# Attention blocks of two to five key tiles, sized freely within each unit, eleven tiles of probabilities, and two steps moved up

## The chip, the cores and the metric

The kernel runs on one core of a Trainium2 chip. The metric is the time of one execution on the device in microseconds (us), the median of several runs. Engine names are those of the profile: PE is TensorE's matmuls and PEld its weight loads, DVE is VectorE, ACT is ScalarE, POOL is GpSimd, SP is SyncE, which here only issues DMAs.

## What is computed

The reference takes 2048 tokens of width 512, normalises each (xn), and computes two branches from xn: attention with 32 heads of 16 columns, and a gated feed-forward network of hidden width 1792. The second branch gates the first.

```python
x = A_x
xn = _layernorm(x, axis=-1)
s = _A_ref(xn, A_wqkv, A_wo)          # softmax(q k^T / 4) v, 32 heads, then @ wo
g = _silu(_B_ref(xn, B_w_gate, B_w_up, B_w_down))   # (silu(xn wg) * (xn wu)) @ wd
return x + s * g
```

## The kernel before

**Prologue.** For each of four blocks of 512 tokens the kernel normalises, transposes and projects to queries, keys and values, and stores the results to DRAM (q_d, k_d, v_d; the normalised, transposed tokens to xt_d). Each float32 operand that needs accuracy is split into a high and a low part, so a product costs three matmuls (high by high, high by low, low by high).

**Attention.** A unit is one group of four heads with one block of 512 queries; there are 32 units, each over 16 key tiles of 128 keys. For one key tile and one j of two (j picks two of the four heads), two score matmuls run side by side on the two 64-row halves of the array and fill score[j], 128 keys x 2 heads x 512 queries in PSUM; ScalarE takes the exponential of it into a tile pr of probabilities (pool ppool, 8 buffers, 4 KB a partition each). So a key tile has two score pairs and two exponentials. The value products (function values) multiply the probabilities by v into the one PSUM tile acc, four heads in four column groups of 32; acc is summed over the 16 key tiles of a unit. Then finish transposes acc on VectorE (L423, in normalise), divides by the sum of probabilities, and for every second group transposes again (L437) and stores to o_d.

**Blocks.** Key tiles are worked in blocks. In a block of k tiles there are 2k score pairs. Between the second and the third score pair the value products of the block before are issued (values(prev)); after the last key tile of a unit, finish follows them. The last score tile of each block writes its second half to the PSUM tile spare, and its exponential is done in two halves (L876, L877), so that the next block's score can start earlier; all others are one instruction (L874). Before, every unit has six blocks, four of three key tiles and two of two (SIZES = {2: 2, 3: 4}), in an order that plan chooses for most of the units.

**Fills.** Into the blocks the kernel weaves the matmuls of the feed-forward network and of the output projection as fills: one call of both is a pair of matmuls on the two 64-row halves, into bankx and banky. The fills come from a queue of generators: ffn for four token blocks (per block 14 tiles of 24 fills for the gate and up weights, then 4 tiles of 24 and 4 of 18 for the down weights), the projection of the last token block's first three parts for two row tiles (EARLY, nine fills each), then project_out for the other three token blocks (twelve fills a tile). plan returns, for each block, its number of key tiles and how many fills follow each score pair from the third on; a tile's end is always a block's end. A tile's results go through ACT and DVE (L264 to L266, split_hidden) or DVE alone (L283, L287).

**Around them.** catch_up carries out work put off in the list after: store_gate (tanh on ACT, a multiplication on DVE, a store by POOL), next_out and load_gates. out_steps loads and splits the operands of the output projection in the last units; its loads of a unit's last part depend on the block's number, now, being past a unit's start. load_gate loads the gate and x rows of the last four row tiles, gate_rest multiplies and adds them for two of these tiles ahead of the end (L407, L408). Key and value chunks of the next head group (load_k, load_v, four key tiles a chunk) are loaded at the end of a block in the last unit of a group, as the chunks come free; queries are loaded a unit ahead. After the last unit the code from L900 normalises it in two halves and finishes the projection of the last token block (L917).

The order on each engine is written out by hand; each engine works its queue in order and waits on semaphores.

Of the kernel before, what the change touches and what calls it, by code (L numbers as in the profile page):

```python
# [38 lines left out]
RING = NB  # L39
DC = D // HALF  # L40
LIMIT = 160.0
SIZES = {2: 2, 3: 4}
FIRST = (4, 0, 4, 3, 3, 2, 2)
EARLY = 2
EPS = 1e-5
# [4 lines left out]
def plan():  # L50

    sizes = sorted(SIZES)
    least, most = {2: 6, 3: 12}, {2: 12, 3: 16}
    left = []
    for i in range(2 * NB):
        nf = GROUPS[i % 2].stop - GROUPS[i % 2].start  # L60
        left += [3 * DC] * nf + [3 * nf] * NT
    left = left[2:]
    blocks = [(3, sum(FIRST)), (2, 3 * DC - sum(FIRST))]
    rest = [3 * (DT - 1)] * EARLY + [3 * DT] * (NT * (NB - 1))
    ends = H // 4 * NB * sum(SIZES.values()) - len(rest)
    whole = tuple(SIZES[k] for k in sizes)
    start = tuple(SIZES[k] - sum(b[0] == k for b in blocks) for k in sizes)
    layers = [{(0, left[0], start): (0, None)}]
    for _ in range(len(blocks), ends):
        new = {}  # L70
        for state, (cost, _) in layers[-1].items():
            tile_no, rem, kinds = state
            kinds = kinds if any(kinds) else whole
            for i, k in enumerate(sizes):
                if not kinds[i]:
                    continue
                for n in range(least[2] // 2, min(most[k], rem) + 1):
                    if n == rem:
                        after = tile_no + 1, left[tile_no + 1] if tile_no + 1 < len(left) else 0
                    elif rem - n >= least[2] // 2:  # L80
                        after = tile_no, rem - n
                    else:
                        continue
                    if after[0] < len(left) or len(layers) + len(blocks) == ends:
                        key = after + (kinds[:i] + (kinds[i] - 1,) + kinds[i + 1:],)
                        c = cost + 100 * max(0, least[k] - n) + abs(n - 4 * k)
                        if key not in new or c < new[key][0]:
                            new[key] = c, (state, k, n)
        layers.append(new)
    state = min((v[0], s) for s, v in layers[-1].items() if s[0] == len(left))[1]  # L90
    kinds = state[2]
    middle = []
    for layer in layers[:0:-1]:
        state, k, n = layer[state][1]
        middle.append((k, n))
    blocks += middle[::-1]
    order = []
    while len(order) < len(rest):
        order += [k for i, k in reversed(list(enumerate(sizes))) for _ in range(kinds[i])]
        kinds = whole  # L100
    blocks += zip(order, rest)
    parts = []
    for k, n in blocks:
        m = 2 * k - 2
        parts.append((k, [0, 0] + [n // m + (i < n % m) for i in range(m)]))
    parts[0] = 3, list(FIRST[1:])
    return parts
# [3 lines left out]
def tile_block(ctx: ExitStack, tc: tile.TileContext, x, wqkv, wo, w_gate, w_up, w_down, out):  # L111
# [239 lines left out]
    def out_steps():  # L351
        for b in range(NB - 1):
            if b not in stage and (len(queue) <= NB, 0 in stage and now > stage.get(0, now), ready[0] == DT)[b]:
                for c in range(DT - 1):
                    load_out(b, c)
                stage[b] = now
            if b in stage and b < 2 and (b, 1) not in stage and now > (u0 + b) * steps:
                load_out(b, DT - 1)
                stage[b, 1] = now
            if b in stage and (b, 2) not in stage and now > stage[b] and (b < 2 or len(queue) <= 2):  # L360
                splits.extend((b, c) for c in range(DT - 1))
                stage[b, 2] = now
                for t in range(0 if b else NT):
                    load_gates(t)
            if (b, 1) in stage and (b, 5) not in stage and now > stage[b, 1]:
                splits.insert(0 if not b else len(splits), (b, DT - 1))
                stage[b, 5] = now
        for _ in range(min(2, len(splits))):
            b, c = splits.pop(0)
            split_o(lhs[b, c], parts_o[b, c])  # L370
            ready[b] += 1
# [34 lines left out]
    def gate_rest(t):  # L406
        dve.scalar_tensor_tensor(facc[:, t], facc[:, t], 0.5, gate[t], op0=ALU.mult, op1=ALU.mult)  # L407
        dve.tensor_add(facc[:, t], facc[:, t], last[t])  # L408


    def values(item):
        u, tiles, probs = item
        for i, kt in enumerate(tiles):
            v = vst[(u // NB * NB + kt // CT) % RING]
            for h in range(4):
                mm(acc[h * 32:h * 32 + DH + 1], v[:, kt % CT, h * (DH + 1):(h + 1) * (DH + 1)],  # L416
                   probs[2 * i + h // 2][:, h % 2], start=kt == 0, stop=kt == KT - 1, skip_group_check=True)
# [14 lines left out]
    def finish(u):  # L432
        g, b = divmod(u, NB)
        normalise(u, 0, TB)
        if g % 2:
            o2 = late.tile([P, TB], F32, tag="o1", name="o2")
            dve.transpose(o2, on[b])  # L437
            if g < NG - 1 or b < 2:
                (pool if g < NG - 1 else sp).dma_start(o_d[g // 2, b], o2)
            else:  # L440
                whole = hh.rearrange("p f j t -> p (f j) t")
                lhs[b, DT - 1] = whole[:, 2 * (DT - 1)], whole[:, 2 * DT - 1]
                split_o(lhs[b, DT - 1], o2)
                ready[b] += 1

    settled = mybir.DependencyInfo(mybir.DependencyClass.Sync, mybir.DependencyReason.DATA)
    units = NG * NB
    steps = sum(SIZES.values())

    u0 = units - NB + 1  # L450

# [17 lines left out]
            given += 1  # L469

    blocks = plan()

    def blocked():
        return not queue or queue[0][0] is not None and ready[queue[0][0]] < DT
# [345 lines left out]
        made()  # L820


    ppool = ctx.enter_context(tc.tile_pool(name="ppool", bufs=8))
    att = ctx.enter_context(tc.tile_pool(name="att", bufs=1))
    late = ctx.enter_context(tc.tile_pool(name="late", bufs=1))
    spool = ctx.enter_context(tc.tile_pool(name="spool", bufs=1, space=PSUM))
# [19 lines left out]
    for u in range(units):  # L846
        g, b = divmod(u, NB)
        q = qst[u % 2]
        kt = 0
        for i in range(steps):  # L850
            now = u * steps + i
            size, parts = blocks[now]
            tiles = range(kt, kt + size)
            kt += size
            probs = []
            if not now:
                fill(FIRST[0])
            for n in range(2 * size):
                t, j = tiles[n // 2], n % 2
                if n == 2:  # L860
                    catch_up()
                    if prev:
                        values(prev)
                        if prev[1][-1] == KT - 1:
                            finish(prev[0])
                k, kc = kst[(g * NB + t // CT) % RING], t % CT

                room, whole = score[j], n < 2 * size - 1
                for h in range(2):
                    r = slice(h * HALF, h * HALF + NROW)  # L870
                    mm(room[:, h] if whole or not h else spare, k[r, j, kc * P:(kc + 1) * P], q[r, j], start=True, stop=True)  # L871
                pr = ppool.tile([P, 2, TB], F32, tag="pr", name="pr")
                if whole:
                    made = act(pr, room, AF.Exp, scale=0.25)  # L874
                else:
                    act(pr[:, 0], room[:, 0], AF.Exp, scale=0.25)  # L876
                    made = act(pr[:, 1], spare, AF.Exp, scale=0.25)  # L877
                exps.append(made)
                if n == 1 and now:
                    tc.add_manual_dep(exps[-1].ins, exps[-3].ins.name, settled, reason="order of the slots' writes")  # L880
                probs.append(pr)
                fill(parts[n])
            if prev and prev[0] // NB + 1 < NG and prev[0] % NB == NB - 1:
                done = prev[1][-1] + 1
                while len(coming) < done // CT:
                    load_k(prev[0] // NB + 1, len(coming))
                    load_v(prev[0] // NB + 1, len(coming))
                    coming.append(now)
                if done == KT:
                    coming.clear()  # L890
            prev = u, tiles, probs
            if i == 0 and u + 1 < units:
                load_q(u + 1)
                load_shift(u + 1)
            out_steps()
            if now == (units - 1) * steps + 1:
                load_gate()
            if 0 <= now - (units - 1) * steps - 4 < EARLY:
                gate_rest(now - (units - 1) * steps - 4)
    values(prev)  # L900
    fill(total)
    catch_up()
# [76 lines left out]
```

## Time and profile before

| what | value |
|---|---|
| median of 3 runs | 1419.76 us (1419.52 to 1419.98) |
| the profiled execution, whole | 1419.49 us |
| its span, first to last instruction | 1417.7 us |
| mean granted TensorE clock | 0.999 |
| attention and fills, 157 to 1403 us | PE busy 1245.45 of 1246.00 us, ACT 1031.38, DVE 452.80 |
| after 1403 us | PE busy 8.49 of 15.00 us, DVE 11.02 |

Busy time is the time in which an engine has an instruction running. Matmuls overlap: a record lasts about 0.39 us, while a pair starts every 0.23 us, so a busy PE may still lose time between starts. The chain of waits gives the distances. A row of the timeline gives the start, the length, the engine and the line of one or several like instructions, and in square brackets the idle time before it and what ended that.

### The profile page before, as it was taken

Reading aid. Unit: us, or ns where it says so; the run is one execution under the profiler, and the core shown is the slowest. Engines: PE = TensorE matmul, PEld = TensorE weight load, DVE = VectorE, ACT = ScalarE, POOL = GpSimd, SP = SyncE. Lnnn points to the kernel's source line nnn. Section 1 sums busy time; section 2 is a strip of 40 time slices with the busy share of each in tenths; the row PEclk is TensorE's granted clock in tenths of the full one; section 3 lists DMA queues with packets and bytes.
Section 4 is the critical chain, followed back from the end, with each engine's and each line's share of the span. In section 5 each row is a group of like instructions: output and inputs, shape, how many; then the busy total and the mean of one; then the engine's idle time right before and its main releaser. Section 6 shows DMA issues by size and latency. Waiting matters only on the chain.

```text
span 1417.7 us, 26890 instructions
## 1 busy us (share of the span) xinstructions
PE 1409.6 (99%) x11197; PEld 817.8 (58%) x11197; DVE 543.2 (38%) x900; ACT 1112.7 (78%) x1427; POOL 90.2 (6%) x102
## 2 busy tenths in 40 slices
PE   9999999999999999999999999999999999999998
PEld 7787655555555555555555555555555555555554
DVE  6643344213423343145224431433244412433645
ACT  6733588888888888878888887888888878888874
POOL 4200100000000000000000000000000000000243
PEclk9999999999999999999999999999999999999999
DMA  7878542042274320242724311256224202313542
GB/s 244 262 247 271 137 95 64 22 96 61 61 159 108 105 75 25 57 110 67 166 65 104 91 39 35 65 124 152 81 64 132 58 12 61 84 54 128 173 153 99
DMA packets 127645, 149.15 MB, mean 105 GB/s; under 512 B 12577, under 2 KB 79649, under 8 KB 126750
## 3 DMA queue, kind: packets, MB, share of 16 engines
q1 hardware_dynamic: 122206, 126.72, 34.7%
q0 software_dynamic: 4880, 20.12, 3.9%
q8 instruction: 90, 1.47, 0.5%
q10 hardware_dynamic: 432, 0.52, 0.1%
q14 instruction: 37, 0.30, 0.1%
HBM read 107.46 MB, written 40.11 MB: 104 GB/s over the span
## 4 chain that ended last, share of the span: by engine, by line
PE 88%; DVE 1%; ACT 0%; issue 0%; DVEq 0%
PE acc L416 32%; PE bankx L235 31%; PE score L871 19%; PE banky L235 5%; PE spare L871 0%; ACT pr L874 0%; PE banky L917 0%; PE score L917 0%; DVE facc L408 0%; DVE o L423 0%; PE spare L917 0%; DVE y L924 0%; DVE y L389 0%; DVE facc L407 0%; DVE y L240 0%
## 5 line engine op out<-in xcount | busy, mean ns | idle before, releaser
L874 ACT ACTIVATE pr<-score 128x1024 f32<-128x1024 f32 x832 | 816.7, 1033 | 201.8 <-PE score L871 190.0
L416 PE MATMUL acc<-pr,vst 128*17 128x512 f32 x4096 | 476.8, 594 | 0.6 <-DVE o L423 0.6
L871 PE MATMUL score<-qst,kst 50*128 50x512 f32 x1856 | 398.2, 418 | 0.0
L871 PEld LDWEIGHTS score<-qst,kst 50*128 50x128 f32 x1856 | 192.9, 184 | 216.4 <-ACT pr L874 153.5
L235 PE MATMUL bankx<-fx,guh 64*128 64x512 f32 x896 | 289.0, 392 | 0.1
L235 PE MATMUL banky<-fx,guh 64*128 64x512 f32 x896 | 289.1, 392 | 0.0
L416 PEld LDWEIGHTS acc<-pr,vst 128*17 128x17 f32 x4096 | 100.5, 97 | 256.4 <-issue 254.5
L235 PE MATMUL banky<-wd,hh 64*128 64x512 f32 x672 | 189.3, 392 | 0.0
L235 PE MATMUL bankx<-wd,hh 64*128 64x512 f32 x672 | 189.3, 392 | 0.0
L235 PEld LDWEIGHTS bankx<-fx,guh 64*128 64x128 f32 x896 | 166.8, 186 | 31.8 <-DVEq L788 0.5
L265 DVE SCALAR_TENSOR_TENSOR ga<-th,bankx 128x512 f32<-128x512 f32 x56 | 38.5, 688 | 371.8 <-ACT th L264 371.8
L235 PE MATMUL banky<-fx,gul 64*128 64x512 f32 x448 | 175.4, 391 | 0.0
L235 PE MATMUL bankx<-fx,gul 64*128 64x512 f32 x448 | 175.3, 391 | 0.0
L235 PEld LDWEIGHTS banky<-fx,guh 64*128 64x128 f32 x896 | 166.8, 186 | 3.4
L235 PEld LDWEIGHTS bankx<-wd,hh 64*128 64x128 f32 x672 | 125.0, 186 | 22.8
L235 PEld LDWEIGHTS banky<-wd,hh 64*128 64x128 f32 x672 | 125.0, 186 | 3.3
L876 ACT ACTIVATE pr<-score 128x512 f32<-128x512 f32 x192 | 114.8, 598 | 11.9 <-PE spare L871 1.8
L877 ACT ACTIVATE pr<-spare 128x512 f32<-128x512 f32 x192 | 114.1, 595 | 0.0
L235 PEld LDWEIGHTS bankx<-fx,gul 64*128 64x128 f32 x448 | 82.8, 185 | 16.0
L235 PEld LDWEIGHTS banky<-fx,gul 64*128 64x128 f32 x448 | 82.9, 185 | 1.9
L626 PE MATMUL ps<-xt,wh 128*128 128x512 f32 x256 | 81.0, 397 | 0.1
L871 PE MATMUL spare<-qst,kst 50*128 50x512 f32 x192 | 75.7, 394 | 0.0
(169 smaller groups left out, 1197.4 us busy)
## 6 DMA issues: line engine op xcount, KB each, us to landing
gur<-in_B_w_gate_dram SPq DMA_DIRECT2D x56, 256.0 KB
gur<-in_B_w_up_dram SPq DMA_DIRECT2D x56, 256.0 KB
wdr<-in_B_w_down_dram SPq DMA_DIRECT2D x56, 256.0 KB
kst<-k_d SPq DMA_DIRECT2D x192, 64.0 KB
qst<-q_d SPq DMA_DIRECT2D x192, 64.0 KB
fx<-xt_d SPq DMA_DIRECT2D x24, 512.0 KB
q_d<-parts SPq DMA_DIRECT2D x16, 512.0 KB
k_d<-parts SPq DMA_DIRECT2D x16, 512.0 KB
```

What stands on the lines that cost most here:

```text
L235: mm(bank, lhs[h], rhs[h], start=start, stop=stop)
L265: dve.scalar_tensor_tensor(ga, th, 1.0, bankx, op0=ALU.add, op1=ALU.mult)
L416: mm(acc[h * 32:h * 32 + DH + 1], v[:, kt % CT, h * (DH + 1):(h + 1) * (DH + 1)], probs[2 * i + h // 2][:, h % 2], start=kt == 0, stop=kt ...
L626: mm(ps, w, a[:, c], start=n == 0, stop=n == 3 * DT - 1)
L871: mm(room[:, h] if whole or not h else spare, k[r, j, kc * P:(kc + 1) * P], q[r, j], start=True, stop=True)
L874: made = act(pr, room, AF.Exp, scale=0.25)
L876: act(pr[:, 0], room[:, 0], AF.Exp, scale=0.25)
L877: made = act(pr[:, 1], spare, AF.Exp, scale=0.25)
```

## The change

Six things are changed.

1. plan is rewritten. Blocks may have 2, 3, 4 or 5 key tiles, any mix that adds up to 16 in a unit and leaves no single tile over. A dynamic programme over (key tiles done, fills done) minimises 1400 per block, 1000 for each fill that a block of k tiles has below 6(k-1), and a small term for uneven shares; a block takes at most 6k+6 fills, at most what is left in the fill tile, and the fills keep within 45 of an even pace. The first two blocks stay. The two nine-fill tiles get two blocks, (2,2), (3,2) or (3,3), whichever is cheapest, and the last two units keep 3, 3, 3, 3, 2, 2.
2. The loop over a unit's blocks and three conditions count from begin, a list of the first block of each unit, in place of multiples of steps.
3. ppool has 11 buffers in place of 8.
4. The size of the scratch memory that the build sets aside for dynamic DMAs is set to 4096 bytes, where no size was given.
5. Where the block before ended a unit, values and finish are issued ahead of catch_up; elsewhere catch_up stays first.
6. gate_rest for the two tiles runs after the fourth and fifth block of the last unit, in place of the fifth and sixth; load_gate stays after the second.

```diff
--- before.py
+++ after.py
@@ -39,7 +39,8 @@
 RING = NB
 DC = D // HALF
 LIMIT = 160.0
-SIZES = {2: 2, 3: 4}
+SIZES = (2, 3, 4, 5)
+LAST = (3, 3, 3, 3, 2, 2)
 FIRST = (4, 0, 4, 3, 3, 2, 2)
 EARLY = 2
 EPS = 1e-5
@@ -53,54 +54,46 @@
 
 
 
-    sizes = sorted(SIZES)
-    least, most = {2: 6, 3: 12}, {2: 12, 3: 16}
-    left = []
+    ends = [0]
     for i in range(2 * NB):
         nf = GROUPS[i % 2].stop - GROUPS[i % 2].start
-        left += [3 * DC] * nf + [3 * nf] * NT
-    left = left[2:]
-    blocks = [(3, sum(FIRST)), (2, 3 * DC - sum(FIRST))]
-    rest = [3 * (DT - 1)] * EARLY + [3 * DT] * (NT * (NB - 1))
-    ends = H // 4 * NB * sum(SIZES.values()) - len(rest)
-    whole = tuple(SIZES[k] for k in sizes)
-    start = tuple(SIZES[k] - sum(b[0] == k for b in blocks) for k in sizes)
...
+        for n in [3 * DC] * nf + [3 * nf] * NT:
+            ends.append(ends[-1] + n)
+
+    ends = [n - ends[1] for n in ends[2:]]
+    first = [(3, sum(FIRST)), (2, ends[0] - sum(FIRST))]
+    units = H // 4 * NB
+    start, stop = sum(k for k, _ in first), (units - 2) * KT
+    pace = (ends[-1] - ends[0]) / (stop - start)
+    short = lambda k, n: 1000 * max(0, 6 * (k - 1) - n)
+    ways = {at: {} for at in range(start, stop + 1)}
+    ways[start][ends[0]] = 0, None
+    for at in range(start, stop):
+        room = KT - at % KT
+        for done, (cost, _) in ways[at].items():
+            rem = next((n for n in ends if n > done), done) - done
+            for k in SIZES:
+                for n in [rem] + list(range(3, rem - 2)):
+                    to = at + k, done + n
+                    if not n or n > 6 * k + 6 or k > room or room - k == 1:
                         continue
-                    if after[0] < len(left) or len(layers) + len(blocks) == ends:
-                        key = after + (kinds[:i] + (kinds[i] - 1,) + kinds[i + 1:],)
-                        c = cost + 100 * max(0, least[k] - n) + abs(n - 4 * k)
-                        if key not in new or c < new[key][0]:
-                            new[key] = c, (state, k, n)
-        layers.append(new)
-    state = min((v[0], s) for s, v in layers[-1].items() if s[0] == len(left))[1]
-    kinds = state[2]
-    middle = []
-    for layer in layers[:0:-1]:
-        state, k, n = layer[state][1]
-        middle.append((k, n))
-    blocks += middle[::-1]
-    order = []
-    while len(order) < len(rest):
-        order += [k for i, k in reversed(list(enumerate(sizes))) for _ in range(kinds[i])]
-        kinds = whole
-    blocks += zip(order, rest)
+                    if abs(to[1] - ends[0] - (to[0] - start) * pace) > 45:
+                        continue
+                    c = cost + 1400 + short(k, n) + 4 * abs(n - 4.1 * k)
+                    if to[1] not in ways[to[0]] or ways[to[0]][to[1]][0] > c:
+                        ways[to[0]][to[1]] = c, (at, done, k, n)
+
+    rest = [3 * (DT - 1)] * EARLY
+    pairs = {4: (2, 2), 5: (3, 2), 6: (3, 3)}
+    cost = lambda r: ways[stop - r][ends[-1]][0] + sum(short(k, n) for k, n in zip(pairs[r], rest))
+    r = min((r for r in pairs if ends[-1] in ways[stop - r]), key=cost)
+    middle, step = [], ways[stop - r][ends[-1]][1]
+    while step:
+        middle.insert(0, step[2:])
+        step = ways[step[0]][step[1]][1]
+    rest += [3 * DT] * (NT * (NB - 1))
     parts = []
-    for k, n in blocks:
+    for k, n in first + middle + list(zip(pairs[r] + 2 * LAST, rest)):
         m = 2 * k - 2
         parts.append((k, [0, 0] + [n // m + (i < n % m) for i in range(m)]))
     parts[0] = 3, list(FIRST[1:])
@@ -354,7 +347,7 @@
                 for c in range(DT - 1):
                     load_out(b, c)
                 stage[b] = now
-            if b in stage and b < 2 and (b, 1) not in stage and now > (u0 + b) * steps:
+            if b in stage and b < 2 and (b, 1) not in stage and now > begin[u0 + b]:
                 load_out(b, DT - 1)
                 stage[b, 1] = now
             if b in stage and (b, 2) not in stage and now > stage[b] and (b < 2 or len(queue) <= 2):
@@ -445,7 +438,6 @@
 
     settled = mybir.DependencyInfo(mybir.DependencyClass.Sync, mybir.DependencyReason.DATA)
     units = NG * NB
-    steps = sum(SIZES.values())
 
     u0 = units - NB + 1
 
@@ -469,6 +461,13 @@
             given += 1
 
     blocks = plan()
+
+    begin, n = [], 0
+    for i, (k, _) in enumerate(blocks):
+        if n % KT == 0:
+            begin.append(i)
+        n += k
+    begin.append(len(blocks))
 
     def blocked():
         return not queue or queue[0][0] is not None and ready[queue[0][0]] < DT
@@ -820,7 +819,7 @@
         made()
 
 
-    ppool = ctx.enter_context(tc.tile_pool(name="ppool", bufs=8))
+    ppool = ctx.enter_context(tc.tile_pool(name="ppool", bufs=11))
     att = ctx.enter_context(tc.tile_pool(name="att", bufs=1))
     late = ctx.enter_context(tc.tile_pool(name="late", bufs=1))
     spool = ctx.enter_context(tc.tile_pool(name="spool", bufs=1, space=PSUM))
@@ -847,8 +846,7 @@
         g, b = divmod(u, NB)
         q = qst[u % 2]
         kt = 0
-        for i in range(steps):
-            now = u * steps + i
+        for now in range(begin[u], begin[u + 1]):
             size, parts = blocks[now]
             tiles = range(kt, kt + size)
             kt += size
@@ -857,12 +855,14 @@
                 fill(FIRST[0])
             for n in range(2 * size):
                 t, j = tiles[n // 2], n % 2
-                if n == 2:
+                if n == 2 and prev and prev[1][-1] == KT - 1:
+                    values(prev)
+                    finish(prev[0])
+                    catch_up()
+                elif n == 2:
                     catch_up()
                     if prev:
                         values(prev)
-                        if prev[1][-1] == KT - 1:
-                            finish(prev[0])
                 k, kc = kst[(g * NB + t // CT) % RING], t % CT
 
                 room, whole = score[j], n < 2 * size - 1
@@ -889,14 +889,14 @@
                 if done == KT:
                     coming.clear()
             prev = u, tiles, probs
-            if i == 0 and u + 1 < units:
+            if now == begin[u] and u + 1 < units:
                 load_q(u + 1)
                 load_shift(u + 1)
             out_steps()
-            if now == (units - 1) * steps + 1:
+            if now == begin[units - 1] + 1:
                 load_gate()
-            if 0 <= now - (units - 1) * steps - 4 < EARLY:
-                gate_rest(now - (units - 1) * steps - 4)
+            if 0 <= now - begin[units - 1] - 3 < EARLY:
+                gate_rest(now - begin[units - 1] - 3)
     values(prev)
     fill(total)
     catch_up()
@@ -962,7 +962,7 @@
     import concourse.bacc as bacc
     from concourse.bass_utils import run_bass_kernel_spmd
 
-    nc = bacc.Bacc("TRN2", target_bir_lowering=False, num_devices=1)
+    nc = bacc.Bacc("TRN2", target_bir_lowering=False, num_devices=1, dynamic_dma_scratch_size=4096)
     arrays, args = {}, []
     for name in _INS:
         a = np.asarray(inputs[name])
```

More of the change, by code (lines that the diff above doesn't have):

```diff
@@ L68, in plan @@
[L68 to L82, printed above, removed]
-                        continue
-                    if after[0] < len(left) or len(layers) + len(blocks) == ends:
-                        key = after + (kinds[:i] + (kinds[i] - 1,) + kinds[i + 1:],)
-                        c = cost + 100 * max(0, least[k] - n) + abs(n - 4 * k)
-                        if key not in new or c < new[key][0]:
-                            new[key] = c, (state, k, n)
-        layers.append(new)
```

## The prediction

> **What bounds the kernel now.** I read the page's first part, then the groups, then the chain of waits in order of time, then PE, ACT and DVE row by row.
>
> ```profile
> span 1417.7 us, 26890 instructions
> PE 1409.6 (99%) x11197; PEld 817.8 (58%) x11197; DVE 543.2 (38%) x900; ACT 1112.7 (78%) x1427; POOL 90.2 (6%) x102
> L874 ACT ACTIVATE pr<-score 128x1024 f32<-128x1024 f32 x832 | 816.7, 1033 | 201.8 <-PE score L871 190.0
> L876 ACT ACTIVATE pr<-score 128x512 f32<-128x512 f32 x192 | 114.8, 598 | 11.9 <-PE spare L871 1.8
> ```
>
> TensorE has work 99% of the span, ScalarE 78%, and ScalarE's idle time ends with a score matmul: TensorE's own order of work is the bound, so only fewer or quicker TensorE steps, or a shorter tail, can shorten the run. The 192 instructions of L876 are one per block (the last score tile of a block is split in two halves), so the kernel runs 192 blocks. How a block is spent, by the chain of waits (start us, length us, what):
>
> ```profile
> 614.50 0.47 PE score L871 x4
> 614.97 2.70 PE acc L416 x24
> 617.67 0.43 PE score L871 x2
> 618.10 0.23 PE bankx L235
> ...
> 620.20 0.47 PE score L871 x4
> 620.67 1.84 PE acc L416 x16
> 622.51 0.43 PE score L871 x2
> 622.94 0.23 PE bankx L235
> ```
>
> A pair of matmuls on the two row halves (one fill, or one score pair) takes 0.23 us. The value products take 2.70 us for three key tiles (x24) and 1.84 for two (x16): 0.86 a tile, and 2.70 − 3 × 0.86 = 0.12 that does not depend on the number of tiles. The first score pair after them takes 0.43 where a pair takes 0.23: 0.20 more. So one change-over from row halves to value products and back costs **0.32 us per block**, in short blocks and long ones alike. That is 192 × 0.32 = 61 us of TensorE's time which computes nothing.
>
> **The change, part by part.**
>
> *Number of blocks.* Every fill, score and value product stays; only the grouping changes. I count the new blocks by hand. The first two (3 and 2 tiles) stay, and so do the last twelve (LAST is the old 3,3,3,3,2,2 in units 30 and 31), with two more ahead of them for the nine-fill tiles. Between lie 512 − 5 − 32 − K' key tiles and 2016 − 24 − 24 = 1968 fills in 70 tiles of 24 and 16 of 18 (each ends with a block). The new planner charges 1400 per block, and 1000 for every fill below 6(k−1) in a block of k tiles. With no fill short, the k−1 of the blocks in a tile of 24 add up to 4 at most (one block of 5, or 4+2, or 3+3), and in a tile of 18 to 3. Over all of them that is 1968/6 = 328 = key tiles − blocks. With K' = 4 (the pair 2,2) there are 471 key tiles, so 471 − 328 = 143 blocks. Saving one more block needs six fills short, 6000 against 1400, and the pair (3,2) in place of (2,2) saves one block for three short fills, 3000: neither pays. That the units' ends at 16 tiles can be met without loss I take from the freedom of 3+3, 4+2 and 5; I did not enumerate it, and allow ±4 blocks. Together 2 + 143 + 2 + 12 = 159 blocks, **33 fewer: 33 × 0.32 = 10.6 us**. A page of the Trainium skill, TensorEngine Tiling (Array Packing), Key Properties, says that changing the tiling mode drains the engine. The trace agrees as far as it goes, with the 0.12 and 0.20 above; the page gives no price.
>
> *ScalarE under longer blocks.* Where the old plan mixed three and four fills between two score pairs, the new one has three almost everywhere, so a score pair comes each 4 × 0.233 = 0.933 us. Can ScalarE follow?
>
> ```profile
> 606.42 0.60 ACT L876 ACTIVATE pr<-score 128x512 f32<-128x512 f32 x1
> 606.91 0.59 ACT L877 ACTIVATE pr<-spare 128x512 f32<-128x512 f32 x1
> 607.60 1.94 ACT L874 ACTIVATE pr<-score 128x1024 f32<-128x1024 f32 x2
> ```
>
> Two exponentials end 1.94 us after the first starts, one lasts 1.03, so they start 0.91 apart; the two halves of the split tile start 0.49 apart, 0.98 together. A block of five therefore needs 7 × 0.91 + 0.98 = 7.35 us for the eight tiles that TensorE hands over in 8 × 0.933 = 7.46. It fits, by 0.1 us. The bounds from rows are 0.91 (no cost) and 1.03 (the whole length, no overlap); I take 0.91, which is the distance itself. ScalarE: Activation LUTs in the Trainium skill (What ACT_TABLE_LOAD costs) speaks against this: 186 ns + 0.833 ns an element less 93 ns of overlap makes an estimate of 0.946 us, over 0.933, some 7 us lost over the run. The 0.91 above disagrees, and the sum goes by it.
>
> *The nine-fill blocks.* What too few fills cost is seen where the old plan put nine fills into blocks of three:
>
> ```profile
> 1314.32 2.77 PE L416 MATMUL acc<-pr,vst 128*17 128x512 f32 x24
> ...
> 1318.76 0.39 PE L871 MATMUL score<-qst,kst 50*128 50x512 f32 x2
> ...
> 1319.57 0.49 PE L871 MATMUL score<-qst,kst 50*128 50x512 f32 x1
> ...
> 1320.49 0.99 PE L871 MATMUL score<-qst,kst 50*128 50x512 f32 x4
> 1321.40 2.77 PE L416 MATMUL acc<-pr,vst 128*17 128x512 f32 x24
> ```
>
> With two fills the pairs should stand 0.70 apart; they stand 0.81 and 0.92. The block lasts 7.08 us; 3 × 0.86 + 15 × 0.233 + 0.32 = 6.40 is its price without waits, so it lost 0.68. The other such block, of the same shape, is counted alike. In blocks of two, nine fills lie four or five to a pair and lose nothing: **1.35 us** gone. Late next there is VectorE's splitting of the projection's operands, in a stretch shorter by two key tiles; I give it nothing and leave 1 us in the range.
>
> *Transposition ahead of the deferred work.* At a unit's end VectorE must read `acc` before the next block's value products may overwrite it. Today the deferred work of catch_up is put into VectorE's queue ahead of it. Once that made TensorE wait (PE row by row):
>
> ```profile
> 1289.54 1.91 PE L416 MATMUL acc<-pr,vst 128*17 128x512 f32 x16 [0.55 <-DVE o L423]
> ```
>
> With values and finish ahead of catch_up, L423 follows the value products at once: **0.55 us** gone. What is queued later in exchange is the gate's multiplication, its POOL store and the splits of next_out, none with a reader near. A second queue can still be in front of L423, a hidden tile's products:
>
> ```profile
> 1209.81 0.69 DVE L206 TENSOR_TENSOR wd<-wdr,wd 128x512 fp32r<-128x512 f32 x1
> 1210.42 0.71 DVE L423 STREAM_TRANSPOSE o<-acc 128x512 f32<-128x512 f32 x1
> ```
>
> Here L423 starts about 1.2 us after the value products' end (3 tiles). Had these been 2 tiles (0.86 us shorter), and the next block the smallest (2 tiles, 6 fills: 10 pairs and the 0.20, 2.5 us), 2.1 + 0.71 would pass 2.5 by 0.3. Five tiles cover it wholly. Cost from 0 to 0.3 us at a few of 31 unit ends; I take 0, and 2 us for the range.
>
> *gate_rest one block earlier.* The tail (DVE, then PE, row by row):
>
> ```profile
> 1403.43 0.68 DVE L407 SCALAR_TENSOR_TENSOR facc<-facc,hh 128x512 f32<-128x512 f32 x1
> 1404.15 1.67 DVE L408 TENSOR_TENSOR facc<-facc,on 128x512 f32<-128x512 f32 x1
> 1405.74 0.43 DVE L423 STREAM_TRANSPOSE o<-acc 128x256 f32<-128x256 f32 x1
> ```
> ```profile
> 1401.85 1.91 PE L416 MATMUL acc<-pr,vst 128*17 128x512 f32 x16
> ...
> 1405.89 0.86 PE L917 MATMUL banky<-fx,part 128*128 128x512 f32 x3
> 1408.15 0.74 PE L917 MATMUL score<-fx,rh 128*128 128x512 f32 x2 [1.40 <-ACT rh L940]
> ```
>
> The value products end at 1403.76, but L423 stands behind L407 and L408 until 1405.74. With these a block earlier it starts at about 1403.85, 1.9 us sooner, and rh with it. TensorE has its own matmuls until 1406.75, the start of the 1.40 us gap, and cannot use more than about that gap: **1.4 us**. A block earlier VectorE has room: it idles most of each of these blocks.
>
> *POOL's scratch, eleven tiles of probabilities.* The smaller scratch makes room for three more tiles. A block of five uses ten, the next block's first two make twelve: one exponential waits for the first of the old tiles, freed some 0.9 us into the value products. It is wanted only after all five (4.4 us), so it is covered; uncovered, 0.9 us a block. The scratch's price no row shows. From one side it is nothing; from the other, a store that holds POOL until it lands:
>
> ```profile
> 21.31 0.92 POOL L705 DMA_DIRECT2D v_d<-vt  x1 [0.70 <-ACT vt L701]
> 22.56 1.28 POOL L533 TENSOR_TENSOR wl<-wraw,wh 128x512 fp32r<-128x512 f32 x1 [0.33 <-ACT wh L529]
> ```
> ```profile
> v_d<-vt POOLq DMA_DIRECT2D x3, 1088.0 KB, 7.4
> ```
>
> Landing takes 7.4 us, issue 0.92; the weights' low parts behind it would come 6.5 us late. I take nothing (issue is POOL's whole part in it now) and keep 6.5 for the range.
>
> *Key and query loads* move with the blocks on SP's queue. A chunk of four key tiles is issued at the latest one block ahead of its first use, 7 us or more; I cost them at nothing.
>
> **Sum.** 10.6 + 1.35 + 0.55 + 1.4 = 13.9 us. The profiled execution took 1419.49 (1417.7 of span, the rest around it); 1419.49 − 13.9 = 1405.6. It stands 0.27 under the median of 1419.76, so I forecast **1405.9**.
>
> **Rivals.**
> 1. *Partial waits eat some of it*: VectorE at unit ends (2 us), operands of the projection (1), four more blocks (1.3), or scores held by ScalarE, whose margin is 0.1 us in a block of five. At the 0.946 of the skill's page, 0.013 × 513 gaps of three fills (two per key tile, 942, less three per block, 429) would be 7 us. The span: 1408 to 1413. For it: the thin margin. Against: the old plan's three-fill stretches run without a wait in the chain above.
> 2. *POOL held by its descriptors in the prologue*: 1405.9 + 6.5 = 1412.4. Nothing in the trace speaks for it but that no row excludes it.
> 3. *Slower: ScalarE becomes the bound.* Its place is the run of eight tiles with three fills each. If the distance were 1.03 there, 513 × 0.10 = 51 us would be lost: 1457. It decides from the point where the lost time passes 13.9 us: 13.9/513 = 0.027, a distance of 0.96. For it: 0.98 for the split tile. Against: 0.91 measured between whole ones, seven of eight.
> 4. *No change*: the 0.32 is not saved, because it reappears in each longer value group or because another chain, such as SP's key loads, ends last: 1417 to 1421. Against: 0.12 comes out from two group sizes, and no chain row has a DMA.
>
> **How the numbers follow.** The forecast (1403.5 to 1408) has 0.66, rival 1 0.16, rival 2 0.04, rival 3 0.06, rival 4 0.05, and better than 1403.5 0.03 (a switch costing up to 0.36, or no gap left in the tail). Low: 0.04 × 33 = 1.3 and 1 us of tail below the forecast, 1403; high: rivals 1 and 2, 1412. This leaves out rivals 3 and 4 and a rest. Faster by over 0.2% (2.8 us, about what a measurement of this kernel can tell from no change) gets 0.89, within 0.05, slower 0.06.
>
> **What would show it.** L876 counts 159, L874 865. A value group of five takes 0.12 + 5 × 0.86 = 4.42 us, and the score pair after it still 0.43. Between score pairs with three fills 0.93, not 0.95 or more. No row like "PE acc waits for DVE o L423". L407 and L408 end ahead of the last value products, and the gap at L917 is gone. It would be wrong if L876 stayed above 165, if weight loads of scores waited for ACT in every long block, or if POOL's stores in the prologue lasted microseconds.

## The result and the profile after

The changed kernel takes 1406.43 us (median of 4 runs, 1406.02 to 1406.69) against 1419.87 (median of 4, 1419.52 to 1420.57): a ratio of 0.9904 with a 95% interval of 0.9887 to 0.9922, 13.4 us less. The forecast was 1405.9 in a range of 1403 to 1412. The profiled execution took 1406.27, with a span of 1404.4.

The page of the changed kernel, its first part, the chain by line, and three groups (value products are now L409 in the code, the transposition of acc L416, gate_rest L400 and L401; the lines from L871 on are as before):

```profile
span 1404.4 us, 26814 instructions
PE 1398.3 (100%) x11197; PEld 826.0 (59%) x11197; DVE 543.2 (39%) x900; ACT 1091.6 (78%) x1394; POOL 90.9 (6%) x102
...
PE acc L409 33%; PE bankx L228 31%; PE score L871 19%; PE banky L228 5%; PE spare L871 0%; PE spare L917 0%; PE banky L917 0%; PE score L917 0%; DVE y L924 0%; DVE y L930 0%; DVEq L975 0%
...
L874 ACT ACTIVATE pr<-score 128x1024 f32<-128x1024 f32 x865 | 836.2, 1032 | 220.4 <-PE score L871 219.2
...
L876 ACT ACTIVATE pr<-score 128x512 f32<-128x512 f32 x159 | 95.0, 598 | 3.1 <-PE spare L871 3.1
```

PE and PEld run as many instructions as before, 11197 each: nothing was taken out of TensorE's work. L876 counts 159, L874 865, as counted by hand: 33 blocks fewer. The chain is TensorE but for the last few us, and L407, L408 and L423 of before, as L400, L401 and L416, are no longer in it.

A block of five in the chain of waits (start, length, what), and ScalarE beside it in the timeline:

```profile
936.51 0.49 PE score L871 x4
937.00 4.42 PE acc L409 x40
941.41 0.43 PE score L871 x2
```
```profile
929.39 6.56 ACT L874 ACTIVATE pr<-score 128x1024 f32<-128x1024 f32 x7 [0.94 <-PE score L871]
935.85 0.59 ACT L876 ACTIVATE pr<-score 128x512 f32<-128x512 f32 x1
936.34 0.59 ACT L877 ACTIVATE pr<-spare 128x512 f32<-128x512 f32 x1
```

Five tiles take 5 × 0.86 + 0.12 = 4.42 us, and the first score pair after them 0.43 again: the change-over costs the same after five tiles as after two. Seven exponentials take 6.56 us, (6.56 − 1.03)/6 = 0.92 apart, close to TensorE's 0.93: ScalarE follows. One figure has grown. The two score pairs ahead of the value products take 0.49 where those of before, quoted in the prediction, took 0.47; the experiments come back to it.

The tail, PE row by row:

```profile
1390.22 1.91 PE L409 MATMUL acc<-pr,vst 128*17 128x512 f32 x16
1392.06 2.37 PE L917 MATMUL spare<-fx,part 128*128 128x512 f32 x9
1394.27 0.86 PE L917 MATMUL banky<-fx,part 128*128 128x512 f32 x3
1394.97 0.63 PE L917 MATMUL score<-fx,rh 128*128 128x512 f32 x2
```

The 1.40 us gap ahead of the rh products is gone. From the start of these last value products to the end of the span it is 1404.4 − 1390.22 = 14.2 us; before it was 1417.7 − 1401.85 = 15.9.

### The profile page after: what moved, and what is told of

The parts are those of the page before. It is cut to its first block, busy times and chain, and to the rows that moved or that the text cites. A ratio compares the mean times of both kernels' runs of the same rounds, so it can differ in the third digit from the quotient of the medians.

```text
span 1404.4 us, 26814 instructions
## 1 busy us (share of the span) xinstructions
PE 1398.3 (100%) x11197; PEld 826.0 (59%) x11197; DVE 543.2 (39%) x900; ACT 1091.6 (78%) x1394; POOL 90.9 (6%) x102
## 4 chain that ended last, share of the span: by engine, by line
PE 89%; DVE 0%; DVEq 0%; issue 0%
PE acc L409 33%; PE bankx L228 31%; PE score L871 19%; PE banky L228 5%; PE spare L871 0%; PE spare L917 0%; PE banky L917 0%; PE score L917 0%; DVE y L924 0%; DVE y L930 0%; DVEq L975 0%
## 5 line engine op out<-in xcount | busy, mean ns | idle before, releaser
L874 ACT ACTIVATE pr<-score 128x1024 f32<-128x1024 f32 x865 | 836.2, 1032 | 220.4 <-PE score L871 219.2
L409 PE MATMUL acc<-pr,vst 128*17 128x512 f32 x4096 | 470.4, 594 | 0.0
L871 PE MATMUL score<-qst,kst 50*128 50x512 f32 x1889 | 400.7, 414 | 0.0
L871 PEld LDWEIGHTS score<-qst,kst 50*128 50x128 f32 x1889 | 193.9, 184 | 192.3 <-ACT pr L874 99.8
L228 PE MATMUL bankx<-fx,guh 64*128 64x512 f32 x896 | 280.5, 392 | 0.1
L228 PE MATMUL banky<-fx,guh 64*128 64x512 f32 x896 | 280.5, 392 | 0.0
L409 PEld LDWEIGHTS acc<-pr,vst 128*17 128x17 f32 x4096 | 103.9, 97 | 259.5 <-issue 258.3
L876 ACT ACTIVATE pr<-score 128x512 f32<-128x512 f32 x159 | 95.0, 598 | 3.1 <-PE spare L871 3.1
L877 ACT ACTIVATE pr<-spare 128x512 f32<-128x512 f32 x159 | 94.4, 593 | 0.0
L276 DVE COPY facc<-bankx 128x512 f32<-128x512 f32 x16 | 11.1, 692 | 155.0 <-PE banky L228 134.9
```

Source lines behind the costliest of these rows:

```text
L228: mm(bank, lhs[h], rhs[h], start=start, stop=stop)
L276: dve.tensor_copy(facc[:, t], bankx)
```

## The experiments

Each run was timed in the same session as runs of the kernel before, which lay between 1419.80 and 1420.06 in the median; times are medians, and "changed" is 1406.43.

| run | what differs | us | ratio to before (95%) |
|---|---|---|---|
| e1_two_three | changed, blocks of 2 and 3 only, 192 blocks | 1415.87 | 0.9971 (0.9961 to 0.9982) |
| e2_mostly_two | changed, 251 blocks | 1432.52 | 1.0088 (1.0071 to 1.0105) |
| e3_short_fills | changed, 133 blocks, 150 fills short | 1433.56 | 1.0098 (1.0081 to 1.0115) |
| e4_many_fives | changed, 159 blocks, 52 of five | 1406.36 | 0.9905 (0.9888 to 0.9921) |
| e9_fives_ten | as e4, ten tiles of probabilities | 1406.48 | 0.9903 (0.9887 to 0.9920) |
| e10_old_order | changed, catch_up first | 1406.58 | 0.9905 (0.9888 to 0.9921) |
| e8_early_threes | changed, nine fills in blocks of 3 | 1407.29 | 0.9910 (0.9893 to 0.9927) |
| e11_late_fill | changed, one fill moved to the last gap | 1405.17 | 0.9897 (0.9880 to 0.9913) |
| e5_gate_only | before, gate_rest earlier | 1418.13 | 0.9989 (0.9979 to 0.9998) |
| e6_finish_only | before, finish ahead of catch_up | 1419.15 | 0.9996 (0.9986 to 1.0005) |
| e7_buffers_only | before, 11 tiles, scratch 4096 | 1419.68 | 0.9999 (0.9989 to 1.0009) |

### The number of blocks: e1_two_three and e2_mostly_two

```diff
-SIZES = (2, 3, 4, 5)
+SIZES = (2, 3)
```


> The changed kernel, but its planner may use blocks of two and three key tiles only; it then gives 192 blocks again, as before, without short fills. Theory (a fixed 0.33 to 0.34 us per block, whatever its size): 33 blocks more than the changed kernel's 159, 33 x 0.335 = 11 us more, 1417.5 us. Rival (the gain came from the buffers, the scratch, the moved steps or the nine-fill blocks, and block sizes matter little): close to 1406 to 1409 us.

```diff
-                    c = cost + 1400 + short(k, n) + 4 * abs(n - 4.1 * k)
+                    c = cost + 1400 + 4000 * (k - 2) + short(k, n) + 4 * abs(n - 4.1 * k)
```


> The changed kernel with a planner that charges 4000 more for each key tile over two in a block: 251 blocks, 241 of them of two tiles. Theory: 92 blocks more than 159, 92 x 0.335 = 31 us more, 1437 us, the same price per block as with 192. Rival (the price is not per block but comes from waits that only some blocks have): well off the line through 159 and 192 blocks, for instance 1420 us, or over 1450 us.

With 16 tiles a unit and only twos and threes, six blocks a unit cannot be undercut, so e1 is back at 192. It took 1415.87 us: 9.4 us more than the changed kernel for 33 blocks, 0.286 each. From 192 to 251 blocks it is 16.65 us for 59, 0.282 each. Three points, one line: the time goes with the number of blocks, and most of the change's gain is this. The rival, that the price comes only from waits that some blocks have, falls. But 0.285 is less than the 0.32 that one block's change-over takes in the chain, and the expected times were 1.6 and 4.5 us too high. The chain of the run with 251 blocks shows what differs:

```profile
606.59 0.46 PE score L871 x4
607.05 1.84 PE acc L409 x16
608.90 0.43 PE score L871 x2
```

Value products (1.84) and the pair after them (0.43) are as everywhere, but the two pairs ahead take 0.46, against 0.49 in the block of five above. The starts of the matmuls in the trace divide a change-over differently from the chain, with nearly the same total: the pair right after the value products takes 0.338 us in the mean in each of these kernels, 0.10 more than the 0.233 of a pair elsewhere, and the other 0.1 falls on the pair right ahead of them. That pair takes 0.327 us in the mean with 251 blocks, 0.341 with e1's 192 and 0.347 with the changed kernel's 159. 250 × 0.327 − 158 × 0.347 is 26.9; at 0.347 throughout it would be 31.9. These 5 us cover the miss of 4.5. For e1 the same sum covers 1.2 of 1.6 (191 × 0.341 − 158 × 0.347 = 10.3 against 33 × 0.347 = 11.5), and the gaps of three fills, 0.932 us in e1 and 0.933 in the changed kernel, point the same way. What the weight loads of the scores waited for is in their group's last column, first of the changed kernel, then of the run with 251 blocks:

```profile
L871 PEld LDWEIGHTS score<-qst,kst 50*128 50x128 f32 x1889 | 193.9, 184 | 192.3 <-ACT pr L874 99.8 <-issue 35.7 <-ACT pr L876 24.1
```
```profile
L871 PEld LDWEIGHTS score<-qst,kst 50*128 50x128 f32 x1797 | 192.2, 184 | 248.3 <-ACT pr L874 213.1 <-ACT pr L876 2.2 <-issue 0.9
```

It is 24.1 us (127 times) against 2.2 us (11 times) of waiting for L876. This is the second score pair of a block: it writes score[1], whose first half the split exponential of the block before has to have read.

### The same wait, taken away: e11_late_fill

```diff
         parts.append((k, [0, 0] + [n // m + (i < n % m) for i in range(m)]))
+        parts[-1][1][2] -= 1
+        parts[-1][1][-1] += 1
```


> The changed kernel with one fill of each block moved from the first gap between score pairs to the last. In the two-tile run the score pair ahead of the value products lasts 0.326 us, in the changed kernel 0.347, and there the weights of that pair wait for the first half of the split exponential 127 times (two-tile run: 11). Theory (a block's price has a part of 0.02 us that comes from this wait): the pair falls to about 0.327, the waits for L876 nearly vanish, 158 x 0.02 = 3 us less than the changed kernel, 1403.4 us. Rival (the pair is longer only because tight blocks follow each other, or the first gap with two fills now stalls for 0.1 us a block): 1406 us, or up to 1422 us.

The split exponential gets one fill, 0.23 us, more ahead of the score that waits for it. The group of the weight loads (L873 here; the split exponential's first half is L878) and a block in the chain:

```profile
L873 PEld LDWEIGHTS score<-qst,kst 50*128 50x128 f32 x1889 | 193.0, 183 | 217.8 <-ACT pr L876 116.1 <-issue 35.7 <-ACT pr L878 4.2
```
```profile
603.20 0.47 PE score L873 x4
603.67 2.70 PE acc L411 x24
```

The waits for the split fall to 4.2 us, and the pair ahead of the value products to 0.333 in the mean (median 0.327), which is 158 × 0.014 = 2.3 us. The time is 1405.17 (1404.95 to 1405.26, no overlap with the changed kernel's runs), 1.3 us less and the fastest kernel of the study, but 1.8 more than the 1403.4 expected. About 1 us of the gain went to the other gaps: those with three fills take 0.935 in the mean where they took 0.933, and the loads' waits for the whole exponentials rose from 99.8 to 116.1 us, as if ScalarE now started each run of tiles a little behind. So the wait is a part of the block's price, as the theory had it; its size was overstated.

The trace of e1 has both kinds of block side by side. The weight loads of the two pairs ahead of the value products run on in the first and are held up in the second (PEld row by row):

```profile
357.30 0.42 PEld L871 LDWEIGHTS score<-qst,kst 50*128 50x128 f32 x4
```
```profile
371.37 0.18 PEld L871 LDWEIGHTS score<-qst,kst 50*128 50x128 f32 x2
371.74 0.19 PEld L871 LDWEIGHTS score<-qst,kst 50*128 50x128 f32 x2 [0.18 <-ACT pr L876]
```

Sorted by when the weight load of the second pair begins, the traces agree. Where it begins more than 0.2 us ahead of its pair, that pair takes 0.326 us in the median of 239 blocks of e2 and 0.327 in 73 of e1. Where it begins less than 0.12 us ahead, the pair takes 0.347 to 0.349, in 10 blocks of e2, 117 of e1 and 152 of the changed kernel. So the three means differ because the share of late loads does, and in e11 only 33 begin so late.

### Too few fills: e3_short_fills and e8_early_threes

```diff
-                    c = cost + 1400 + short(k, n) + 4 * abs(n - 4.1 * k)
+                    c = cost + 8000 + short(k, n) + 4 * abs(n - 4.1 * k)
```


> The changed kernel with a planner that charges 8000 per block instead of 1400: 133 blocks, 59 of them of five tiles, but 150 fills short of three per gap in 28 of the blocks. Theory (ScalarE needs 0.91 us per score pair, TensorE waits out what is short, 0.22 us per missing fill, as in the nine-fill blocks): 26 x 0.335 = 9 us saved, 150 x 0.22 = 33 us lost, 1430 us. Rival (ScalarE makes up what is short while the value products of five tiles run): 1397 to 1402 us, and fewer blocks would be better still.

```diff
-    pairs = {4: (2, 2), 5: (3, 2), 6: (3, 3)}
+    pairs = {6: (3, 3)}
```


> The changed kernel with blocks of three forced on the two nine-fill tiles: 157 blocks, six fills short in these two. Theory: six fills short at 0.22 us are 1.35 us lost, two blocks fewer at 0.29 us are 0.6 us saved, 1407.1 us, and these two blocks last 7.08 us as in the kernel before. Rival (the wait there was for the operands of the projection, not for ScalarE): no such loss, 1405.8 us.

With 26 blocks fewer still, e3 lost 27.1 us. 26 × 0.285 = 7.4 were saved, so 34.5 were lost over 150 missing fills, 0.23 each. Not all of it is waiting. In one block with hardly any fills, where TensorE stands idle up to 0.41 us at a time, the granted clock of the profiled run falls to 0.68 (from 1160 to 1170 us), and the value products of five tiles take 5.81 where such a row has 4.49 elsewhere in this trace:

```profile
1163.61 5.81 PE L409 MATMUL acc<-pr,vst 128*17 128x512 f32 x40
```

The mean clock is 0.997 in all four runs, against 0.999 to 1.000 in the changed kernel's. For the clock an estimate from these figures is 1.3 us (the excess of this group) to 3.2 us (0.32 of the ten), which leaves 0.21 to 0.22 us for each missing fill, nearly a fill's whole time; why the clock fell is not shown. Score pairs of another of its blocks, PE row by row:

```profile
710.12 0.40 PE L871 MATMUL score<-qst,kst 50*128 50x512 f32 x2
710.82 0.40 PE L871 MATMUL score<-qst,kst 50*128 50x512 f32 x2
711.64 0.50 PE L871 MATMUL score<-qst,kst 50*128 50x512 f32 x2
712.55 0.51 PE L871 MATMUL score<-qst,kst 50*128 50x512 f32 x2
713.47 0.50 PE L871 MATMUL score<-qst,kst 50*128 50x512 f32 x2
```

The first gap with two fills is 0.70, the second 0.82, then 0.91 to 0.92: after two gaps ScalarE sets the pace, and that pace is the distance of 0.91 read from its rows before. Five tiles of value products make up nothing of it; as I read it, because only the two score tiles are there for ScalarE to work on meanwhile. In e8 the two nine-fill blocks of three behave as in the kernel before: the score pairs of the first lie 0.72, 0.81 and 0.91 apart.

```profile
1300.32 0.40 PE L871 MATMUL score<-qst,kst 50*128 50x512 f32 x2
1301.04 0.40 PE L871 MATMUL score<-qst,kst 50*128 50x512 f32 x2
1301.85 0.50 PE L871 MATMUL score<-qst,kst 50*128 50x512 f32 x1
...
1302.76 0.99 PE L871 MATMUL score<-qst,kst 50*128 50x512 f32 x4
1303.68 2.77 PE L409 MATMUL acc<-pr,vst 128*17 128x512 f32 x24
```

The time is 0.86 us more than the changed kernel's: six fills at 0.23 less two blocks at 0.285 would be 0.81. The difference is near what the runs can tell (the kernel before took 0.19 us more in e8's session than in the changed kernel's); the rows are the firmer part.

### Blocks of five and their buffers: e4_many_fives, e9_fives_ten, e7_buffers_only

```diff
-                    c = cost + 1400 + short(k, n) + 4 * abs(n - 4.1 * k)
+                    c = cost + 1400 - 300 * (k == 5) + short(k, n) + 4 * abs(n - 4.1 * k)
```


> The changed kernel with a planner that likes blocks of five: still 159 blocks and no short fills, but 52 of five tiles in place of 13. Theory (eleven tiles of probabilities suffice, ScalarE's 0.1 us of margin in a block of five holds): within 1 us of the changed kernel, 1406 us, gaps of three fills at 0.93 us. Rival (each block of five costs a wait of ScalarE for a probability tile that TensorE then sees, 0.3 us or more): 39 x 0.3 = 12 us more, 1418 us.

e9 adds to this:

```diff
-    ppool = ctx.enter_context(tc.tile_pool(name="ppool", bufs=11))
+    ppool = ctx.enter_context(tc.tile_pool(name="ppool", bufs=10))
```


> The kernel with 52 blocks of five, with ten tiles of probabilities in place of eleven. Theory (the wait of the next block's first exponentials for a tile is covered by the value products of five tiles, 4.4 us): both of the next block's first exponentials now wait, about 1 us into the value products, and nothing is late: 1406.4 us as with eleven. Rival (the cover is thin, the eleventh tile is needed): 52 x 0.3 to 0.9 us more, 1422 to 1453 us.

e7 is the kernel before with these two edits:

```diff
-    ppool = ctx.enter_context(tc.tile_pool(name="ppool", bufs=8))
+    ppool = ctx.enter_context(tc.tile_pool(name="ppool", bufs=11))
...
-    nc = bacc.Bacc("TRN2", target_bir_lowering=False, num_devices=1)
+    nc = bacc.Bacc("TRN2", target_bir_lowering=False, num_devices=1, dynamic_dma_scratch_size=4096)
```


> The kernel before, with eleven tiles of probabilities and 4096 bytes of scratch, nothing else. Theory: blocks of three need eight tiles, so no difference; POOL's stores take 0.9 and 0.5 us to issue as before: 1419.9 us. Rival (the smaller scratch holds POOL in the prologue until its stores land): up to 6.5 us more, 1426 us, with v_d stores that last several us on POOL.

39 more blocks of five in place of other sizes, at the same number of blocks, changed nothing (1406.36), and neither did the eleventh tile (1406.48 with ten). The list of waits of e4, then of e9 (engine, line, what it waited for; total us, times, longest):

```profile
ACT pr L874 <- PE acc L409: 2.7, 12, 0.2
```
```profile
ACT pr L874 <- PE acc L409: 39.7, 52, 1.1
```

With ten tiles ScalarE waits once in each block of five for the value products to free a tile, 0.8 us in the mean, and TensorE does not see it: a wait of 39.7 us in total that costs nothing. e7 took 1419.68, and POOL's rows in its prologue are those of before:

```profile
21.26 0.92 POOL L705 DMA_DIRECT2D v_d<-vt  x1 [0.69 <-ACT vt L701]
22.51 1.28 POOL L533 TENSOR_TENSOR wl<-wraw,wh 128x512 fp32r<-128x512 f32 x1 [0.32 <-ACT wh L529]
```

The store still takes 0.92 us of POOL. The smaller scratch held nothing up.

### The two steps moved up: e5_gate_only, e6_finish_only, e10_old_order

```diff
-            if 0 <= now - (units - 1) * steps - 4 < EARLY:
-                gate_rest(now - (units - 1) * steps - 4)
+            if 0 <= now - (units - 1) * steps - 3 < EARLY:
+                gate_rest(now - (units - 1) * steps - 3)
```


> The kernel before, with gate_rest alone one block earlier. Theory: the transposition of the last unit no longer stands behind L407 and L408, TensorE's 1.40 us gap in the tail goes, 1.4 to 1.7 us less than before (1418.3 us) and nothing else changes. Rival (the tail is bound by TensorE's products or by the two late blocks, which now carry VectorE's additions): within 0.3 us of before.

```diff
-                if n == 2:
+                if n == 2 and prev and prev[1][-1] == KT - 1:
+                    values(prev)
+                    finish(prev[0])
+                    catch_up()
+                elif n == 2:
                     catch_up()
                     if prev:
                         values(prev)
-                        if prev[1][-1] == KT - 1:
-                            finish(prev[0])
```


> The kernel before, with values and finish ahead of catch_up at a unit's end, nothing else. Theory: the one wait of TensorE for L423 goes, 0.6 us less than before (1419.3 us), no such wait anywhere. Rival (the work put off is then late for its own readers): the wait goes, but another appears behind it, in the splits for the projection, and the time stays at 1419.9 us or above.

e10 is the changed kernel with this last edit undone.

> The changed kernel with catch_up ahead of values and finish again at a unit's end. Theory (the order matters only where deferred work meets the end of a unit ahead of a short block, as once in the kernel before): 1406.4 to 1407 us, with at most one or two rows in which PE or its weight load waits for L416's transposition. Rival (the new plan, with its blocks of two at units' ends, meets this more often): several such waits, 1408 us or more.

e5 took 1.67 us less than before, and its tail, PE row by row, has no gap:

```profile
1405.96 0.87 PE L917 MATMUL banky<-fx,part 128*128 128x512 f32 x3
1406.67 0.63 PE L917 MATMUL score<-fx,rh 128*128 128x512 f32 x2
```

e6 took 0.65 us less. Its interval includes no change, so the reading rests on the rows. The list of waits of the kernel before has these two, that of e6 has neither:

```profile
PEld acc L416 <- DVE o L423: 0.9, 1, 0.9
...
PE acc L416 <- DVE o L423: 0.6, 1, 0.6
```

In e10, with the old order back in the changed kernel, no wait of PE for L416 appears either, and the time is 1406.58, 0.15 more, in a session in which the kernel before was 0.19 slower. So either the new order (e6) or the new plan (e10) alone removes that wait, and within the changed kernel the new order is worth nothing that can be measured.

## Why the prediction was right, point by point

- **The bound.** Right. TensorE carried the chain before and after, and every edit that changed the time did so through TensorE's order, through what makes it wait (e3, e8), or through the tail.
- **33 blocks fewer.** The count was exact, 159, and no fill is short. The price of a block was mis-sized: 0.32 read from the chain and taken as fixed, 0.286 measured between e1 and the changed kernel, so 9.4 us instead of 10.6. Counted by the starts of the matmuls, the 0.12 of the value products and the 0.10 of the pair after them are fixed, in every run and with 2 to 5 tiles. The pair ahead of the value products is not: it grows from 0.327 to 0.347 as the gaps tighten to three fills, so that each block saved makes those that stay a little dearer. The prediction saw how thin ScalarE's margin is, and looked for it in the gaps, where 538 gaps of three fills take 0.933 in the mean as forecast; it appeared at the block's end, where a weight load waits for the split exponential. In that small way a part of rival 1 came true: scores held by ScalarE.
- **ScalarE under longer blocks.** Right: 0.91 to 0.92 apart, and TensorE's gaps stayed at 0.933. The estimate of 0.946 from the Trainium skill, ScalarE: Activation LUTs (What ACT_TABLE_LOAD costs), is refuted here by that 0.91 to 0.92. Rival 3 falls with e4; its point of decision was real, since e3 shows 0.92 setting the pace once the gaps are shorter. One sign of being wrong was badly chosen: weight loads of scores do wait for ACT in 25 of 28 blocks of four and 9 of 13 of five (counting waits over 0.15 us), but so they did in 124 of 127 blocks of three before. Where nothing holds it up, a load of the second pair begins 0.23 us ahead of its matmuls (e1), and most of its wait never reaches them.
- **Nine-fill blocks.** Right as far as it can be told, 1.35 us: e8 brings the waits back, and its net 0.86 us fits.
- **Transposition.** The stall was real and worth 0.65 us in the kernel before by e6's median, on an interval that includes no change. That it is gone the prediction put down to the order alone; the new plan would have removed it without the order (e10), which the prediction did not see. The size was right, the attribution only half.
- **gate_rest.** 1.4 forecast, 1.67 measured (e5). The gap of 1.40 went whole, and the products after it follow more closely too.
- **Buffers and scratch.** Nothing, as forecast (e7, e9); rival 2 falls, and rival 4 with the measured time.

9.4 from the sizes of blocks, and 1.35 + 0.65 + 1.67 = 3.7 from the three smaller edits, make 13.1 of the 13.4 us. That e1 stands 4.1 us under the before of its own session, with 192 blocks as there, says the same. The forecast of 13.9 was half a microsecond high: the blocks' term was too high by 1.2, and the small terms were too low by 0.4 by their sum, or by 0.8 by e1. That the total came closer than its largest term is luck, two errors of opposite sign.

What stays open is how a late weight load lengthens its pair. A load lasts 0.18 us, so one that begins 0.08 us ahead ends after the pair has begun, by the trace; but only 0.02 us of a wait of 0.19 us reaches the value products, and no row shows why it is that much.

## What to carry to other kernels

When one engine is busy all the time, look for time that does nothing within its order of work: here a change-over that costs the same for two tiles as for five, so that each group fewer is worth 0.29 us. Price it from two group sizes, and then find what limits the size of a group (here another engine's pace, 0.91 us against 0.93), since a group over that limit loses nearly a fill's whole time (0.21 to 0.23 us of 0.23) for each fill missing. Where the last work of a group hands over to the next, leave the other engine a little room: moving one fill from the first gap to the last, with nothing else changed, gave another 1.3 us.

## What the runs showed that was not expected

The price of a change-over depends on the slack of another engine: the last pair takes 0.327 us where its weights are loaded early and 0.348 where late, with no idle time of PE in the profile, since a matmul's record of 0.39 us hides it. And a wait can be long and free: 39.7 us of ScalarE waiting for value products in e9 left the time where it was.
